# Moving four sums of step 1 from VectorE to GpSimd and to a transfer

## The chip, the cores and the metric

The kernel runs on one NeuronCore of one Trainium2 chip. The metric is the device time of one execution in microseconds. Five engines work side by side, each through its own queue in program order: TensorE (PE in the profile, its weight loads PEld), VectorE (DVE), ScalarE (ACT), GpSimd (POOL) and SyncE (SP), which here only issues transfers. GpSimd issues transfers as well, among them those that add to what stands at their destination. All transfers share 16 transfer engines.

## The reference

```
x_pad = concatenate([zeros((B, K-1, D)), x], axis=1)        # B=8, S=4096, D=192, K=7
out = einsum('hk,bskhg->bshg', softmax(weight), windows(x_pad))   # causal convolution, 8 heads
h = out.reshape(B*S, D) @ w_in                               # 192 -> 2048
g = h * (1 / (1 + exp(-1.702 * h)))
y = g @ w_out                                                # 2048 -> 192
```

A short convolution along the sequence, the same taps for the 24 channels of a head, then two matrix products with a gelu between them, over 32768 tokens, all in float32.

## The kernel before

The tokens are cut into 32 tiles of 1024, one step each (`big` = 0 to 31). Step 0 fills the pipeline and prepares the weights; the loop at the end of the kernel runs steps 1 to 31. Each step has two stages.

`hidden` is the first stage: `h` and its gelu. The blocks of `h` are not computed one by one but from 41 products of sums of blocks of the convolved input with sums of blocks of `w_in`; they are accumulated in four pairs of PSUM banks (`p0` to `p3`), copied, and combined by joins. The order of all this is written out by hand in the list `HIDDEN` (line 737): `mm` is a product (TensorE, L709), `copy` moves a pair of banks (ScalarE L802 or VectorE L804), `join` adds or subtracts two pairs (VectorE, L817), `gelu` writes two rows of `g` (ScalarE, L826 and L833), `early` adds rows of `g` for the next stage. One of the 41 products, `fetch`, already belongs to the next step.

`second` is the second stage: the product with `w_out`, again from sums, of blocks of `g` with sums of blocks of `w_out` (`form`, in `w_out_s` and `w_form`). 25 main products of up to four matmul groups each run one after the other beside side products (TensorE, L1207). Their order stands in `PLAN` (line 1143): `sum` is a sum of blocks of `g` on VectorE (L435 for a plus, L437 for a minus), `acc` the same as an adding transfer from GpSimd's queue (L1183), `seed` and `join` combine results, `tap` multiplies the input of a later step's convolution by one coefficient on ScalarE (L570), `piece` is a piece of the next step's sums of convolved blocks, `turn` and `store` write the output.

The blocks are numbered homes, `spot(i)`: 0 and 1 are the halves of `osbs`, 2 to 4 are rows of `room`, 5 to 20 are the 16 blocks of `g`, each of 128 partitions x 1024 elements. Homes that are free for a while also hold other things: 0 and 1 are `k7` and `k8` of `hidden`, 2 is `k0`.

Some of these sums stand in `hidden` already, in `EARLY_G` (line 1139), which `early(i)` reads; each item is (destination, operand, operation, operand). The last, `(8, 0, "acc")`, is an adding transfer in steps 2 to 31. Step 1 has a list of its own, `EARLY_G_1`, in which that item is a sum on VectorE, so all six are on VectorE in step 1. The places of `early` in `HIDDEN` run 0, 3, 4, then 1 and 5 together, then 2. In `second`, the second `sum` of the plan reads home 8, the fourth main product reads home 0, and the second `side` product, which runs beside it, reads home 1.

Step 1 differs from the later ones. The convolution of its successor's middle third is not finished when it begins: `middle_tap(k)` multiplies one tap on ScalarE (L1096), and a tree of six additions, `middle_pairs`, puts the seven results together. The first addition is on VectorE (L1116), the others are adding transfers (L1114) that `middle_tree(n)` issues, the last two where the third `turn` of `HIDDEN` stands. Work that is to run beside the joins waits in the list `beside`; each join takes one piece from it. Until the third `turn`, `held` keeps back what concerns the next step's convolution (`over`, `ve`, `vc`), in the list `waiting`; then `over` runs, and the rest is released by `last_turn`, the second piece of `beside` after that turn. `ve(i)` is a sum of convolved blocks on GpSimd (L437, `conv_t`), `vc(b)` a copy across partition halves by two transfers from SyncE's queue (L609).

## Time and profile before

| | |
|---|---|
| median of 3 runs | 2263.79 us (2263.47 to 2264.4) |
| the profiled execution's own time | 2263.37 us |
| its span, first to last instruction | 2261.7 us |
| TensorE busy | 2249.5 us |
| VectorE, ScalarE busy | 2112.6, 1714.5 us |
| GpSimd busy | 989.3 us |
| granted TensorE clock | 1.00 |

Every row of the profile says what ran where: start and duration in microseconds, engine, line, operation, the tiles written and read, and in brackets how long the engine had been idle before and what ended that. Matmuls overlap, and their ends are modelled, so a gap in their issue shows only in part as idle time. GpSimd's spans are rough. A view of one engine in the order of time merges neighbours of one kind ("x5"). The first stage of step 1 lies at 93.6 to 136.3 us from the span's start, its second stage at 136.3 to 173.2.

### The profile page before, as it was taken

The numbers are of one execution on the slowest core, as the hardware profiler recorded it, in microseconds if no ns is written. First come the engines' busy times: TensorE is split into PE (matmuls) and PEld (weight loads), VectorE is DVE, ScalarE is ACT, GpSimd is POOL, SyncE is SP. The second block draws the span as 40 slices with busy tenths as digits, with TensorE's granted clock in tenths as the row PEclk, the third lists the DMA queues.
The fourth block names the chain that finished last, engine by engine and source line by source line (L and its number), as shares of the span: only waits on it lengthen the run. The fifth ranks groups of instructions, "written<-read, shape, count | busy, mean of one in ns | idle before, by whom it ended". The sixth has DMA issues, their size and how long they took to land.

```text
span 2261.7 us, 63910 instructions
## 1 busy us (share of the span) xinstructions
PE 2249.5 (99%) x25090; PEld 1348.2 (60%) x25090; DVE 2112.6 (93%) x3266; ACT 1714.5 (76%) x3342; POOL 989.3 (44%) x1013
## 2 busy tenths in 40 slices
PE   9999999999999999999999999999999999999999
PEld 5455655666656666566665566665666656666655
DVE  8999999999999999999999999999999999999998
ACT  8777787777877777777778777777777877777844
POOL 1544454354543444544445434454344454344510
PEclk9999999999999999999999999999999999999999
DMA  9997768866778767787666886677876768765743
GB/s 205 181 173 144 147 134 162 160 139 138 143 150 169 142 138 146 140 165 152 138 141 136 159 164 141 136 144 147 172 142 138 148 134 165 157 137 113 138 96 71
DMA packets 340988, 330.45 MB, mean 146 GB/s; under 512 B 130161, under 2 KB 279281, under 8 KB 340689
## 3 DMA queue, kind: packets, MB, share of 16 engines
q0 software_dynamic: 66928, 168.65, 42.3%
q1 hardware_dynamic: 272112, 157.32, 30.3%
q8 instruction: 199, 3.26, 0.6%
q14 instruction: 101, 0.82, 0.1%
q10 hardware_dynamic: 1648, 0.39, 0.1%
HBM read 53.15 MB, written 25.17 MB: 35 GB/s over the span
## 4 chain that ended last, share of the span: by engine, by line
PE 96%; DVE 2%; ACT 1%; DMA 1%; issue 0%; POOL 0%; SPq 0%; DVEq 0%; ACTq 0%; POOLq 0%
PE slot L709 37%; PE slot L1207 28%; PE sums L1207 17%; PE sums L709 13%; PE slot L987 1%; DVE g L437 0%; DMA g<-g 0%; PE sums L992 0%; DVE g L817 0%; PE slot L992 0%; DMA xin<-in_x_dram 0%; ACT g L833 0%; DVE xt L518 0%; ACT g L826 0%; DVE room L437 0%
## 5 line engine op out<-in xcount | busy, mean ns | idle before, releaser
L709 PE MATMUL slot<-conv_t,w_in_s 64*128 64x512 f32 x3372 | 826.6, 593 | 1.3 <-ACT slot L802 0.7
L1207 PE MATMUL slot<-g,w_form 128*32 128x256 f32 x5872 | 713.5, 379 | 0.0
L709 PEld LDWEIGHTS slot<-conv_t,w_in_s 64*128 64x128 f32 x3372 | 451.1, 187 | 285.2 <-issue 178.6
L437 DVE TENSOR_TENSOR g<-g 128x1024 f32<-128x1024 f32 x372 | 445.0, 1224 | 9.2 <-ACT g L833 1.9
L1207 PE MATMUL sums<-g,w_form 128*32 128x256 f32 x3800 | 422.0, 379 | 0.0
L1207 PEld LDWEIGHTS slot<-g,w_form 128*32 128x32 f32 x5872 | 365.3, 110 | 89.4
L826 ACT ACTIVATE g<-slot 128x512 f32<-128x512 f32 x494 | 265.1, 625 | 127.9 <-PE slot L709 126.5
L709 PE MATMUL sums<-conv_t,w_in_s 64*128 64x512 f32 x1284 | 350.1, 593 | 0.5 <-ACT osbs L802 0.3
L1207 PE MATMUL slot<-g,w_out_s 128*32 128x256 f32 x4080 | 321.5, 380 | 2.4 <-DVE g L437 1.7
L1183 POOL DMA_DIRECT2D g<-g x124 | 116.4, 939 | 441.7 <-PE slot L1207 302.9
L1232 ACT COPY room<-slot 32x256 f32<-32x256 f32 x434 | 158.5, 365 | 188.7 <-PE slot L1207 174.6
L570 ACT ACTIVATE g<-xt,cw 128x512 f32<-128x512 f32 x389 | 270.3, 719 | 4.8 <-PE slot L992 0.4
L437 POOL TENSOR_TENSOR conv_t<-conv_t 128x256 f32<-128x256 f32 x209 | 195.5, 953 | 156.9 <-PE slot L709 90.6
L1207 PEld LDWEIGHTS sums<-g,w_form 128*32 128x32 f32 x3800 | 211.7, 110 | 69.3
L1207 PEld LDWEIGHTS slot<-g,w_out_s 128*32 128x32 f32 x4080 | 166.1, 110 | 128.5 <-ACT g L826 11.4
L915 POOL TENSOR_TENSOR conv_t<-conv_t,g 128x512 f32<-128x512 f32 x174 | 238.6, 1392 | 4.5
L709 PEld LDWEIGHTS sums<-conv_t,w_in_s 64*128 64x128 f32 x1284 | 171.9, 187 | 106.0 <-issue 58.2
L833 ACT ACTIVATE g<-g 128x1024 f32<-128x1024 f32 x155 | 170.7, 1101 | 0.0
L915 POOL TENSOR_TENSOR g<-g 128x512 f32<-128x512 f32 x87 | 110.7, 1273 | 122.7 <-ACT g L570 120.5
L1232 ACT COPY room<-sums 32x256 f32<-32x256 f32 x217 | 79.3, 366 | 103.6 <-PE sums L1207 91.4
L709 PE MATMUL slot<-g,w_in_s 64*128 64x512 f32 x556 | 150.6, 590 | 0.2 <-DVE slot L817 0.2
L826 ACT ACTIVATE g<-sums 128x512 f32<-128x512 f32 x188 | 103.9, 616 | 58.0 <-PE sums L709 57.5
(254 smaller groups left out, 3912.2 us busy)
## 6 DMA issues: line engine op xcount, KB each, us to landing
g<-g POOLq DMA_DIRECT2D x124, 512.0 KB, 6.5
conv_t<-conv_t SPq DMA_DIRECT2D x844, 64.0 KB, 2.0
xin<-in_x_dram SPq DMA_DIRECT2D x240, 180.0 KB, 6.2
out_dram<-osbs SPq DMA_DIRECT2D x183, 128.0 KB, 2.5
g<-g POOLq DMA_DIRECT2D x65, 256.0 KB, 6.7
g<-g SPq DMA_DIRECT2D x248, 64.0 KB, 3.6
g<-room POOLq DMA_DIRECT2D x31, 512.0 KB, 6.0
g<-osbs POOLq DMA_DIRECT2D x30, 512.0 KB, 6.4
```

The lines of the kernel that those rows point to most:

```text
L437: eng.tensor_sub(v(dst), v(a), v(b))
L570: act.mul(home, conv_src(big, c, k), cw[:, c, k : k + 1])
L709: nc.tensor.matmul(slot[h], w_in_s[halves[h], a, v * P : (v + 1) * P], src, start=first, stop=True, skip_group_check=True,)
L826: act.activation(dst[:, :, h, :], ot(bank(src, h)), AF.Gelu_apprx_sigmoid, scale=float(sign))
L833: act.activation(dst.rearrange("p o h t -> p h o t"), src, AF.Gelu_apprx_sigmoid, scale=float(sign))
L915: (vec if eng == "v" else nc.gpsimd).tensor_add(dst, dst, home)
L987: nc.tensor.matmul(chunk(bank, c), w[:, chunk_cols(c)], t, start=first and i == 0, stop=not more and i == len(steps) - 1, skip_group_check ...
L1183: nc.gpsimd.dma_start(out=spot(dst), in_=spot(a), accum_op=ALU.add)
L1207: nc.tensor.matmul(dst, w, t, start=first, stop=last, skip_group_check=True)
L1232: act.copy(to, d)
```

## The change

All of it concerns step 1 (`big == 1`) alone.

- The sum into home 6 (`early(0)`) is issued behind the join into `o10` instead of ahead of it.
- The sum into home 0 (`early(3)`) stays on VectorE. Behind it, the sum into home 8, which was the last but one on VectorE, becomes an adding transfer from home 0.
- The sum into home 2 (`early(4)`) and the two into home 1 (`early(1)`, `early(2)`) go to GpSimd.
- Of the tree's last two additions, which are transfers, one is issued at the third turn as before and the other three pieces of `beside` later. On GpSimd's queue the order is thus: transfer of the tree, transfer into home 8, sum into home 2, last transfer of the tree, two sums into home 1, then the five sums of convolved blocks.
- The held work (`ve`, `vc`) is released when `HIDDEN` is through, instead of within `last_turn`.
- The taps 2 and 3 of the middle third, and with them the addition on VectorE behind tap 3, are issued behind ScalarE's copy of `p3` into `p2`, instead of during the joins ahead of it.

The order of the instructions on TensorE and on SyncE is the same in both kernels; VectorE has four fewer, GpSimd four more.

```diff
@@ copy @@
             if eng == "v" and after_copy:
                 after_copy.pop(0)()
+            if (dst, src) == ("p2", "p3"):
+                while late_taps:
+                    middle_tap(late_taps.pop(0))
@@ join @@
+            if big == 1 and dst == "o10":
+                sum_g(*LATE_G_1)
             seen_joins.append(0)
@@ turn @@
                 held.append(0)
-                middle_tree(2)
+                middle_tree(1)
                 next_turn()
 
-                def last_turn():
-                    next_turn()
-                    held.clear()
-                    while waiting:
-                        waiting.pop(0)()
-
-                beside.extend([next_turn, last_turn, lambda: need("forms")])
+                def last():
+                    need("forms")
+                    middle_tree(1)
+
+                beside.extend([next_turn, next_turn, last])
@@ early @@
-            for item in (EARLY_G if big > 1 else EARLY_G_1)[i]:
-                sum_g(*item)
+            if big > 1:
+                for item in EARLY_G[i]:
+                    sum_g(*item)
+            else:
+                for eng, *item in EARLY_G_1[i]:
+                    sum_g(*item, eng=eng)
@@ hidden, at its end @@
-        assert not beside
+        assert not beside and not late_taps
+        held.clear()
+        while waiting:
+            waiting.pop(0)()
@@ second_first @@
                 sums_w_in(FETCH[0], 3 + 2 * j, 5 + 2 * j)
-                if 0 < j <= K:
+                if j in (3, 4):
+                    late_taps.append(j - 1)
+                elif 0 < j <= K:
                     middle_tap(j - 1)
@@ the lists @@
-    EARLY_G_1 = EARLY_G[:5] + [[(8, 8, "+", 0)]]
+    EARLY_G_1 = [
+        [], [(nc.gpsimd, 1, 7, "-", 6)], [(nc.gpsimd, 1, 1, "-", 11)],
+        [(vec, 0, 5, "+", 6), (None, 8, 0, "acc")], [(nc.gpsimd, 2, 9, "-", 0)], [],
+    ]
+    LATE_G_1 = (6, 6, "-", 10)
@@ sum_g @@
-    def sum_g(dst, a, op, b=None):
+    def sum_g(dst, a, op, b=None, eng=None):
 
         if op == "acc":
             nc.gpsimd.dma_start(out=spot(dst), in_=spot(a), accum_op=ALU.add)
         else:
-            add_up(spot, dst, a, op, b)
+            add_up(spot, dst, a, op, b, eng=eng or vec)
```

More of the change, by code (lines that the diff above doesn't have):

```diff
@@ L1084, in more @@
                 sums_w_in(FETCH[0], 3 + 2 * j, 5 + 2 * j)
-                if 0 < j <= K:
+                if j in (3, 4):
+                    late_taps.append(j - 1)
+                elif 0 < j <= K:
                     middle_tap(j - 1)
             beside.append(more)
-    after_copy, beside = [], []
+    after_copy, beside, late_taps = [], [], []
     MIDDLE = ((14, 0), (11, 2), (3, 0), (17, 2), (3, 2), (11, 2))
```

## The prediction, as it stood before the changed kernel was run

> **What bounds the kernel now.** I read the page first, then the stretches of single stages, then the order of time of each engine around step 1, and the chain that ended last there.
>
> ```profile
> span 2261.7 us, 63910 instructions
> PE 2249.5 (99%) x25090; PEld 1348.2 (60%) x25090; DVE 2112.6 (93%) x3266; ACT 1714.5 (76%) x3342; POOL 989.3 (44%) x1013
> ```
>
> TensorE sets the time: it is busy for 99% of the span. An edit can win only where TensorE stands still, so the next view cuts the span at the stage borders (first the products through L709, then those through L1207) of step 1, and of steps 2 and 3 for comparison.
>
> ```profile
> 93.60:136.28 42.68, 41.19 (x167) 1.00 0.98 185
> 136.28:173.18 36.90, 34.47 (x626) 1.00 1.00 191
> 209.30:243.11 33.81, 33.81 (x626) 1.00 0.98 181
> 243.11:278.75 35.64, 35.64 (x169) 1.00 0.52 115
> ```
>
> The columns are the stretch, its length, TensorE's busy time and matmuls, the granted clock (1.00 throughout) and the transfers' share and rate. A later first stage takes 35.64 us, 41 products and half of one at the border, so 0.859 us a product; that of step 1 takes 42.68, 7.0 more. A later second stage takes 33.81; that of step 1 takes 36.90, 3.1 more. These 10.1 us are all that step 1 can give. Where they lie, by the idle time in brackets:
>
> ```profile
> 112.85 5.55 PE L709 MATMUL slot<-conv_t,w_in_s 64*128 64x512 f32 x23 [0.68 <-ACT slot L802]
> 119.88 4.76 PE L709 MATMUL slot<-conv_t,w_in_s 64*128 64x512 f32 x19 [0.19 <-ACT g L826]
> 129.92 3.44 PE L709 MATMUL slot<-conv_t,w_in_s 64*128 64x512 f32 x12
> 132.90 1.30 PE L709 MATMUL sums<-conv_t,w_in_s 64*128 64x512 f32 x3
> 140.84 0.42 PE L1207 MATMUL slot<-g,w_out_s 128*32 128x256 f32 x3 [0.91 <-DVE g L437]
> 142.59 1.91 PE L1207 MATMUL sums<-osbs,w_form 128*32 128x256 f32 x32
> 145.32 0.42 PE L1207 MATMUL slot<-g,w_out_s 128*32 128x256 f32 x3 [0.82 <-DVE g L437]
> 171.31 0.42 PE L1207 MATMUL slot<-g,w_out_s 128*32 128x256 f32 x3 [0.70 <-DVE room L435]
> ```
>
> The three waits of the second stage make its 3.1 us: about 1.1, 1.1 and 0.9, each some 0.2 over its bracket, because a matmul's modelled end hides the first part of a gap.
>
> **The taps behind the copy.** ScalarE's order was tap (110.03), gelu, a second such tap, copy (112.21):
>
> ```profile
> 110.03 0.73 ACT L1096 ACTIVATE g<-xt,cw 128x512 f32<-128x512 f32 x1
> 110.65 1.05 ACT L833 ACTIVATE g<-g 128x1024 f32<-128x1024 f32 x1
> ...
> 112.21 1.07 ACT L802 ACTIVATE slot<-slot 128x512 f32<-128x512 f32 x2
> ...
> 118.22 2.09 ACT L826 ACTIVATE g<-slot 128x512 f32<-128x512 f32 x4
> ...
> 135.16 2.06 ACT L826 ACTIVATE g<-slot 128x512 f32<-128x512 f32 x4
> ```
>
> With both taps after it, the copy starts at 111.0, 1.2 earlier, and TensorE's product at 112.85 starts near 111.6. The taps still lie ahead of the same gelu, so from 113.2 on ScalarE is where it was, and TensorE's wait at 119.88 is for the gelus that start at 118.22: there the 1.2 us are given back. The addition at L1116 on VectorE now waits for the late tap and pushes the join behind it by 0.43, which VectorE's idle 0.78 before 115.38 takes up (without that cover it would cost 0.43). I put this edit at 0.
>
> **The sums on VectorE.**
>
> ```profile
> 115.38 1.30 DVE L817 TENSOR_TENSOR sums<-osbs,g 128x512 f32<-128x512 f32 x2 [0.78 <-ACT g L826]
> 118.40 1.23 DVE L437 TENSOR_TENSOR g<-g 128x1024 f32<-128x1024 f32 x1 [0.59 <-ACT g L833]
> 126.20 1.18 DVE L435 TENSOR_TENSOR osbs<-g 128x1024 f32<-128x1024 f32 x1
> 131.05 1.19 DVE L437 TENSOR_TENSOR room<-g,osbs 128x1024 f32<-128x1024 f32 x1
> 132.16 1.29 DVE L817 TENSOR_TENSOR sums<-g,room 128x512 f32<-128x512 f32 x2
> 134.55 1.22 DVE L437 TENSOR_TENSOR osbs<-g 128x1024 f32<-128x1024 f32 x1
> 135.69 1.75 DVE L435 TENSOR_TENSOR g<-g,osbs 128x1024 f32<-128x1024 f32 x1
> 137.36 1.76 DVE L437 TENSOR_TENSOR osbs<-osbs,g 128x1024 f32<-128x1024 f32 x1
> 139.04 7.49 DVE L437 TENSOR_TENSOR g<-g 128x1024 f32<-128x1024 f32 x5
> ```
>
> The sum at 118.40 goes behind the join that followed it. Both orders stand idle until about 118.4, once for the gelu and once for the product that the join reads, so it is worth 0, or 0.1.
>
> The sum at 131.05 leaves: the join behind it starts 1.11 earlier. TensorE's three products from 129.92 should end at 132.50 and the next one starts at 132.90; it waits for that join. Gain 0.4, and the second stage starts at 135.9.
>
> The sums at 134.55, 135.69 and 137.36 leave: 4.5 us. VectorE is through its last join at 133.4 and then waits for the gelu whose two halves are the first half of the row at 135.16: until 136.2, less the 0.4, so 135.8. The five sums could start 3.2 earlier than 139.04, the waits at 140.84 and 145.32 would be gone, and the stage would come 2 to 3 us shorter. That is the gain to be had; what follows is what it costs elsewhere.
>
> **What GpSimd gets.** Its queue, with the moved work to come between the first two rows (a transfer, a sum) and after the second (two sums), ahead of the five sums of `conv_t`:
>
> ```profile
> 126.75 0.86 POOL L1114 DMA_DIRECT2D room<-room  x1 [4.68 <-issue]
> 130.57 0.86 POOL L1114 DMA_DIRECT2D conv_t<-room  x1 [2.96 <-issue]
> 135.19 7.86 POOL L437 TENSOR_TENSOR conv_t<-conv_t 128x256 f32<-128x256 f32 x5 [3.77 <-DMA xin<-in_x_dram]
> 143.09 0.87 POOL L1183 DMA_DIRECT2D g<-g  x1
> ```
>
> The groups of GpSimd's sums from step 2 on (the first number behind the bar is the busy time, the second the mean in ns), and the page's median from issue to landing of a transfer of 512 KB:
>
> ```profile
> L915 POOL TENSOR_TENSOR g<-g 128x512 f32<-128x512 f32 x87 | 110.7, 1273 | 122.7 <-ACT g L570 120.5
> L437 POOL TENSOR_TENSOR g<-conv_t 128x256 f32<-128x256 f32 x30 | 22.0, 734 | 6.6 <-PE slot L1207 6.6
> ```
> ```profile
> g<-g POOLq DMA_DIRECT2D x124, 512.0 KB, 6.5
> ```
>
> No row has a GpSimd sum of 1024 elements. One of 256 takes 0.73, one of 512 takes 1.27, so 0.54 for each further 256: 2.4 for 1024, if nothing disturbs it. Beside VectorE's sums the five of 256 took 7.86, near 1.7 each once VectorE's sums are under way, and VectorE's took 1.75 instead of 1.2: 1.7 is VectorE's 1.15 (a sum's way to the next start, 1.11 at 131.05) and GpSimd's 0.55 one after the other. If a long sum suffered in proportion, 2.3 times, it would take 5.6. I take 2.4, with one such sum standing in VectorE's way, because most of VectorE's work in these microseconds has an operand in PSUM or is idle time.
>
> [...]
>
> So: the transfer g<-osbs is issued when the sum at 126.20 is done, 127.4; the first sum runs 128.6 to 131.0, the transfer conv_t<-room follows, the second sum waits for the join of two SBUF operands until 132.3 and ends at 134.6, the third at 137.0. The transfer (6.5 us to landing) has landed by 134.5, before the second of VectorE's five sums needs it. The product at 142.59 reads the third sum; it comes at 141.1 now, 4 us of cover. VectorE's first sum ends at 138.1, the fourth at 143.2; TensorE wants that at 142.8 and waits 0.4. GpSimd's five sums end at 138.1 + 0.55 + 4 x 1.7 = 145.5, not 143.05; with 2.4 us sums everywhere and no contest it would be near 141, in proportion throughout near 155. SyncE's copies of `conv_t` wait for these sums and go with them; they are wanted only in step 2.
>
> **Who waits for GpSimd.** The transfer at 143.09 goes behind those five sums. The chain that ended last in step 1:
>
> ```profile
> 156.20 10.28 DMA g<-g
> 166.60 0.43 DVE g L437
> ```
>
> A transfer issued at 156.20 lands 10.28 us later; VectorE waits for it, TensorE's wait at 171.31 is 4.7 behind that, the end of the stage 1.9 more. So the end hangs on this landing, and 10.28 against a median of 6.5 says that it stood in line:
>
> ```profile
> 142.00:144.00 2.00, 2.00 (x44) 1.23 (x40) 2.00 (x2) 0.64 (x2) 1.92 (x2) 1.00 0.36 88
> 144.00:146.00 2.00, 1.18 (x25) 0.44 (x20) 1.97 (x3) 1.34 (x3) 0.00 (x0) 1.00 0.87 168
> 148.00:150.00 2.00, 2.00 (x44) 1.23 (x40) 2.00 (x3) 1.39 (x3) 0.86 (x1) 1.00 0.64 150
> ```
>
> The second number from the right is the share of the 16 transfer engines: 0.36 with SyncE's copies alone, 0.87 once the transfer of 143.09 moves (some 1.5 us after its issue), full from 150 on. Unused from 142 to 150 (146 to 148 counted as full): 2 x (0.64 + 0.13 + 0.36) = 2.3 us. Afterwards the same bytes have to pass. With the issue at 145.5 and its bytes from 147.0, 5.0 x 0.64 = 3.2 us stay unused, after which the line is full, since VectorE and ScalarE are early and issue is no limit: the landing comes 0.9 later, and the stage ends 0.9 later, whatever TensorE and VectorE won before it. The balance is at an issue near 144.0 (3.5 x 0.64 = 2.3); 1.6 us later costs another 1.
>
> **Sum.** 2263.4 (the profiled execution's own time, span 2261.7) + 0.9 = 2264.3; the median of the runs, 2263.79, lies 0.4 above that execution, so 2264.7.
>
> **Rivals.** *The line of transfers doesn't decide.* If the long sums pass quicker and GpSimd issues by 141 to 143, or the copies' delay thins the line, the landing moves with VectorE: 1 to 2.6 us earlier, at most all of 0.4 + 3.1 = 3.5. For it: 4 us of cover on the third sum, and a full second stage of 33.81 in step 2 with the same transfers. Against it: the two-fold slowing that the rows show just here. About 2.2 won, 2261.6.
>
> *GpSimd becomes the bound.* Should the three long sums end after 141.1, TensorE waits at the product that reads the third. At that point the five short sums end at 149.6 and the line starts at 151.1: 9.1 x 0.64 - 2.3 = 3.5 us lost; at 5.6 us a sum, 146.3, it is 5.2 on that wait and up to 9 at the end. For it: the 1.7 in place of 0.73; against it: VectorE's idle time and PSUM joins beside them. About 5 lost, 2268.8.
>
> *The change moves work but nothing on the path*, the gain in the first stage swallowed at the end of the second and the line as before: 2263.8. This lies within the forecast's own range.
>
> **How the numbers follow.** The forecast, with its neighbour of no effect, 0.53 (2263.2 to 2266.3); the gain, 0.31; GpSimd as the bound, 0.16. The range 2261.2 to 2267.8 holds the first, some two thirds of the second and a third of the third. A change of 0.2%, about 4.5 us, is what a measurement here can tell from none. A gain over 4.5 exceeds the 3.5 worked out: 0.03. A loss over it needs the worse half of the third case and a little besides: 0.12. Within: 0.85.
>
> **What would show it.** TensorE's idle before 140.84 gone and that before 145.32 at most 0.4; the one at 119.88 unchanged; the second stage starting at about 135.9; GpSimd's long sums at 2.4 to 3.4; the transfer now at 143.09 issued near 145.5, and VectorE waiting several microseconds, not 1.1, for the landing near 167.4. Wrong would be a second stage of 34 us without that wait (the gain), a long idle time of TensorE at a product that reads `osbs` (GpSimd), or stalls in step 2, which I take as unchanged.

## The result and the profile after

The changed kernel takes 2267.69 us (median of 22 runs, 2266.71 to 2270.22), the kernel before 2263.83 (median of 22 runs beside it, 2262.76 to 2265.32). The ratio of the means is 1.0019, with a 95% interval of 1.0013 to 1.0026: slower, by 3.9 us between the medians. The 22 times of the changed kernel lie in two groups, 14 from 2266.71 to 2267.96 and 8 from 2269.18 to 2270.22; the profiled execution is of the first, and what the others lose besides isn't shown by any trace. The forecast was 2264.7. Unless another kernel is named, "after" is the changed kernel and all times in us count from the start of the span of the profiled execution; that of after has a span of 2266.0 and a time of 2267.71, 4.34 more than that of before. In after's numbering the copy is still L802, the join is L820, the gelus are L831 and L838, the tree's transfers L1126, the accumulating transfers L1199, the second stage's products L1223.

The stages first: the first stage of step 1 from its second product, its second stage, and a piece of the first one. The columns are the stretch, its length, the busy time of TensorE, its weight loads, VectorE, ScalarE and GpSimd with their instructions, then the granted clock and the share and rate of the transfers.

```profile
93.52:143.29 49.77, 44.29 (x167) 22.94 (x164) 43.40 (x77) 37.82 (x70) 28.14 (x28) 0.97 1.02 193
143.29:177.09 33.80, 33.80 (x625) 20.17 (x624) 30.78 (x48) 24.71 (x52) 11.21 (x13) 1.00 0.93 178
...
138.60:142.00 3.40, 2.92 (x8) 1.38 (x9) 1.61 (x3) 0.81 (x2) 3.40 (x5) 0.50 1.16 220
```

The second stage got all that was to be had there: 33.80 instead of 36.90, 3.1 won. The first stage lost 7.1 (42.68 before). The first stage of step 2 is 0.5 shorter (35.64 against 36.12); a first stage much later in the span is 0.9 longer; the rest is alike to a tenth of a microsecond. 7.1 - 3.1 - 0.5 + 0.9 = 4.4, the difference of the two profiled times.

Where the first stage stood still, in TensorE's order of time:

```profile
111.54 2.46 PE L709 MATMUL slot<-conv_t,w_in_s 64*128 64x512 f32 x8
...
117.73 2.04 PE L709 MATMUL slot<-conv_t,w_in_s 64*128 64x512 f32 x7 [0.98 <-ACT osbs L802]
...
131.27 3.44 PE L709 MATMUL slot<-conv_t,w_in_s 64*128 64x512 f32 x12
136.33 1.12 PE L709 MATMUL sums<-conv_t,w_in_s 64*128 64x512 f32 x2 [1.63 <-DVE sums L820]
139.08 1.22 PE L709 MATMUL sums<-conv_t,w_in_s 64*128 64x512 f32 x1 [1.63 <-DVE sums L820]
```

The product that reads the join `sums<-g,room` waits twice, once for each half of it. The three products from 131.27 should end at 133.85; the next starts at 136.33. VectorE's row of that join, then GpSimd's order:

```profile
132.40 6.63 DVE L820 TENSOR_TENSOR sums<-g,room 128x512 f32<-128x512 f32 x2
```
```profile
129.82 2.69 POOL L437 TENSOR_TENSOR room<-g,osbs 128x1024 f32<-128x1024 f32 x1
132.13 1.21 POOL L1126 DMA_DIRECT2D conv_t<-room  x1
132.73 2.98 POOL L437 TENSOR_TENSOR osbs<-g 128x1024 f32<-128x1024 f32 x1
135.79 2.68 POOL L437 TENSOR_TENSOR osbs<-osbs,g 128x1024 f32<-128x1024 f32 x1
138.43 3.91 POOL L437 TENSOR_TENSOR conv_t<-conv_t 128x256 f32<-128x256 f32 x5
148.99 0.87 POOL L1199 DMA_DIRECT2D g<-g  x1 [6.65 <-PE slot L1223]
```

The join took 1.29 before and takes 6.63. GpSimd's second long sum ends at 132.73 + 2.98 = 135.71, its third at 138.47; each half of the join is done 0.57 behind one of these ends, and a matmul follows 0.05 later. Two of the expectations below call that exclusion. While GpSimd's first long sum ran, VectorE's join that reads one operand from PSUM (`slot<-slot,room`, at 130.54) took its usual 1.27. The chain that ended last goes through this join, too.

From 138.60 to 142.01 TensorE's clock was at half (the row 138.60:142.00 above, 0.50). From 139.08 on, pairs of matmuls came every 0.85 or more instead of 0.43: four such steps took 3.26, to 142.34, instead of 1.72, which costs another 1.5. The first stage of before shows 1.00 throughout.

The remaining 1.35 were lost earlier. TensorE's product at 117.73 waits for ScalarE's copy `osbs<-slot`, which before ran at 115.71 without a wait:

```profile
117.09 1.07 ACT L802 COPY osbs<-slot 128x512 f32<-128x512 f32 x2 [1.35 <-PE slot L709]
```
```profile
L1149 SPq DMA_DIRECT2D out_dram<-osbs x3: 315/586/1158, 106.2 to 108.4; - x3
...
DMA to landing us min/median/max: 3.6/6.1/8.5
```

The second fence is the view of the tile `osbs` between 104 and 119 us: its transfers with the first and the last start, and their time to landing. The TensorE product that the copy reads had ended long before, so the releaser named is not the true one. The copy overwrites `osbs`, which SyncE's three transfers to `out_dram` read. In before they land 4.3 to 4.9 us after their issue, in after 3.6 to 8.5; the one that takes 8.5 is the last, which starts at 108.4, so it lands at 116.9, just ahead of the copy.

From 131.27 to its end the first stage of after takes 12.02 us; in before the same work, from 129.92 on, took 6.36. Of the 5.7 lost here the clock has 1.5; the other 4.2 are the two gaps, beyond the 0.4 that before lost at this place.

### The profile page after: what moved, and what is told of

It is laid out like the page before. It is cut to its first block, busy times and chain, and to the rows that moved or that the text cites. A ratio compares the mean times of both kernels' runs of the same rounds, so it can differ in the third digit from the quotient of the medians.

```text
span 2266.0 us, 63915 instructions
## 1 busy us (share of the span) xinstructions
PE 2252.9 (99%) x25090; PEld 1350.1 (60%) x25090; DVE 2111.7 (93%) x3262; ACT 1715.2 (76%) x3342; POOL 993.2 (44%) x1017
## 3 DMA queue, kind: packets, MB, share of 16 engines
q8 instruction: 199, 3.26, 0.6%
## 4 chain that ended last, share of the span: by engine, by line
PE 94%; DMA 2%; DVE 2%; issue 1%; ACT 0%; SPq 0%; POOL 0%; DVEq 0%; POOLq 0%
PE slot L709 35%; PE slot L1223 29%; PE sums L1223 17%; PE sums L709 12%; DMA g<-g 1%; DMA g<-in_moe_w_in_dram 1%; DMA w_form<-w_out_s 0%; DMA w_form<-w_form 0%; SPq L340 0%; DVE sums L820 0%; DVE xt L518 0%; POOL g L600 0%; POOL conv_t L600 0%; DMA conv_t<-g 0%; SPq L99 0%
## 5 line engine op out<-in xcount | busy, mean ns | idle before, releaser
L1223 PE MATMUL slot<-g,w_form 128*32 128x256 f32 x5872 | 713.0, 379 | 0.0
L1223 PE MATMUL sums<-g,w_form 128*32 128x256 f32 x3800 | 422.0, 379 | 0.0
L1223 PEld LDWEIGHTS slot<-g,w_form 128*32 128x32 f32 x5872 | 364.4, 110 | 89.8
L831 ACT ACTIVATE g<-slot 128x512 f32<-128x512 f32 x494 | 265.2, 625 | 128.2 <-PE slot L709 126.8
L1223 PE MATMUL slot<-g,w_out_s 128*32 128x256 f32 x4080 | 321.3, 379 | 0.0
L1199 POOL DMA_DIRECT2D g<-g x124 | 116.2, 937 | 452.8 <-PE slot L1223 300.4
L1248 ACT COPY room<-slot 32x256 f32<-32x256 f32 x434 | 158.4, 365 | 186.2 <-PE slot L1223 172.2
L1223 PEld LDWEIGHTS sums<-g,w_form 128*32 128x32 f32 x3800 | 211.1, 110 | 69.5
L1223 PEld LDWEIGHTS slot<-g,w_out_s 128*32 128x32 f32 x4080 | 166.2, 110 | 125.4 <-ACT g L831 11.4
L838 ACT ACTIVATE g<-g 128x1024 f32<-128x1024 f32 x155 | 170.6, 1101 | 0.0
L831 ACT ACTIVATE g<-sums 128x512 f32<-128x512 f32 x188 | 104.0, 615 | 63.6 <-PE sums L709 59.9
```

The costliest lines, as they stand in the source:

```text
L831: act.activation(dst[:, :, h, :], ot(bank(src, h)), AF.Gelu_apprx_sigmoid, scale=float(sign))
L838: act.activation(dst.rearrange("p o h t -> p h o t"), src, AF.Gelu_apprx_sigmoid, scale=float(sign))
L1199: nc.gpsimd.dma_start(out=spot(dst), in_=spot(a), accum_op=ALU.add)
L1223: nc.tensor.matmul(dst, w, t, start=first, stop=last, skip_group_check=True)
L1248: act.copy(to, d)
```

## The experiments

Twelve kernels, each against the kernel before on the same chip. The first column of numbers is the median, then the ratio to before with its 95% interval, then the join `sums<-g,room` and the end of the second stage of step 1 in the profiled execution:

```
                        median us   ratio (95%)                join us   stage ends
before                  2263.5-2263.95                           1.29      173.18
after                   2267.69     1.0019 (1.0013 to 1.0026)    6.63      177.09
e1_home1_vec            2263.84     1.0002 (0.9993 to 1.0010)    2.57      175.63
e2_quarters             2272.23     1.0035 (1.0022 to 1.0047)   10.93      182.65
e3_taps_alone           2263.20     0.9997 (0.9988 to 1.0006)    1.29      173.16
e4_home1_gps_alone      2266.94     1.0013 (1.0005 to 1.0022)    1.29      177.91
e5_transfer_alone       2263.16     0.9999 (0.9990 to 1.0008)    1.29      172.85
e6_conv_vec             2262.53     0.9996 (0.9987 to 1.0005)    1.29      173.18
e7_pairs                2269.73     1.0027 (1.0016 to 1.0037)    3.58      179.97
e8_tree_first           2263.73     1.0000 (0.9991 to 1.0009)    1.29      172.31
e9_no_issue_ahead       2267.64     1.0017 (1.0007 to 1.0027)    2.35      178.02
e10_less_line           2262.92     0.9996 (0.9987 to 1.0006)    1.29      172.09
e11_no_transfer         2263.35     1.0000 (0.9991 to 1.0008)    1.29      172.87
e12_issue_behind        2269.87     1.0027 (1.0017 to 1.0037)    5.73      178.54
```

### e1: the two sums into home 1 back on VectorE

```
-        [], [(nc.gpsimd, 1, 7, "-", 6)], [(nc.gpsimd, 1, 1, "-", 11)],
+        [], [(vec, 1, 7, "-", 6)], [(vec, 1, 1, "-", 11)],
```

> The changed kernel with its two long sums into home 1 (`osbs<-g`, `osbs<-osbs,g`) back on VectorE behind its last join; the sum into home 2 stays on GpSimd, the sum into home 8 stays a transfer. Theory (a join of two SBUF operands stands for one whole GpSimd sum in each of its halves): the join `sums<-g,room` takes 1.3 us again instead of 6.63, TensorE's gaps of 2.6 and 2.7 us in front of the last products of the first stage are gone, the granted clock stays 1.00, the second stage stays near 33.8 to 34.3 (it was 36.90 before, 33.80 after), since the two sums fit into VectorE's wait for the last gelus. Time 2260.3 (2263.8 less 0.4 and 3.1) to 2261.8 (if the 1.35 us at the copy `osbs<-slot` come again). Rival (the loss of 3.9 us comes from the moved taps, or from transfers that land later, and the long join only fills time that was lost already): 2264 or more, with TensorE still waiting somewhere near 136 to 139.

The loss is gone: no difference to before. GpSimd's one long sum that is left still holds the join, whose first half was ready at 131.3 and is done 0.56 behind that sum's end at 132.61. VectorE's and GpSimd's rows:

```profile
131.21 2.57 DVE L820 TENSOR_TENSOR sums<-g,room 128x512 f32<-128x512 f32 x2
```
```profile
129.73 2.88 POOL L437 TENSOR_TENSOR room<-g,osbs 128x1024 f32<-128x1024 f32 x1
...
139.10 7.89 POOL L437 TENSOR_TENSOR conv_t<-conv_t 128x256 f32<-128x256 f32 x5 [5.66 <-DMA conv_t<-room]
146.93 0.87 POOL L1199 DMA_DIRECT2D g<-g  x1
```

The clock stays at 1.00. The time missed its 2260.3 to 2261.8, though: VectorE's five sums start at 137.34, 1.7 earlier than before, and the stage doesn't win it. In this execution (span 2264.0, so some 2 us over the runs' median) the sums of `conv_t` wait for the tree's last transfer, the accumulating transfer behind them goes at 146.93 instead of 143.09, and the chain that ended last goes through one transfer, 2.45 later than the 166.48 of before:

```profile
155.44 13.49 DMA g<-g
```

So the loss of after is the join that waits for GpSimd, as the theory had it, and in this execution the gain that should then show is taken by the line of transfers.

### e2: the same two sums in quarters

```
+            cuts = 4 if dst == 1 and eng is nc.gpsimd else 1
+            n = NG // cuts
+            for q in range(cuts):
+                add_up(lambda s: spot(s)[:, q * n : (q + 1) * n, :], dst, a, op, b, eng=eng or vec)
```

> The changed kernel with each of GpSimd's two long sums into home 1 cut into four of 256 elements. Theory (the join's half waits for the one GpSimd instruction under way, and gets its turn behind it): the join `sums<-g,room` takes 1.3 plus at most 2 x 0.75, so 2 to 2.8 us instead of 6.63, the clock stays 1.00, the first stage comes 3.5 to 5 us shorter than the changed kernel's 50.7, time 2262 to 2264. Rival (GpSimd holds VectorE off for as long as it has sums queued, whatever their length): the join still takes 5 to 7 us and the time is 2267 to 2268.5. Rival 2 (no exclusion, the join waits for data or a buffer): unchanged at 6.6 us, 2267.7.

The theory as written fell: shorter instructions made it worse. The first half of the join stood from 132.41 to 142.74, through all thirteen sums that GpSimd had in its queue, of which the last ended at 142.17:

```profile
132.41 10.93 DVE L820 TENSOR_TENSOR sums<-g,room 128x512 f32<-128x512 f32 x2
```
```profile
132.13 1.20 POOL L1126 DMA_DIRECT2D conv_t<-room  x1
132.74 3.37 POOL L437 TENSOR_TENSOR osbs<-g 128x256 f32<-128x256 f32 x4
135.47 3.33 POOL L437 TENSOR_TENSOR osbs<-osbs,g 128x256 f32<-128x256 f32 x4
138.19 3.98 POOL L437 TENSOR_TENSOR conv_t<-conv_t 128x256 f32<-128x256 f32 x5
```

The rows overlap: the first four quarters last from 132.74 to 136.11, and the next row starts at 135.47, 0.64 earlier; so does the third. GpSimd's next sum always started before the last had ended, and VectorE got in behind the last of them only: its first half was done 0.57 after that sum's end. In before the same five sums of `conv_t` took turns with VectorE's sums (7.86 for the five). The rival, that a queued row of GpSimd holds VectorE off, is right here, and not there.

### e7 and e9: what opens the row

In e7 each quarter of the first sum is followed by the quarter of the second that reads its result; GpSimd has to wait for itself after every other sum.

```
...
+        for q in range(4):
+            cut = lambda s: spot(s)[:, q * n : (q + 1) * n, :]
+            add_up(cut, 1, 7, "-", 6, eng=nc.gpsimd)
+            add_up(cut, 1, 1, "-", 11, eng=nc.gpsimd)
```

> The changed kernel with GpSimd's two long sums into home 1 cut into four quarters of 256 elements as in the run with quarters, but in pairs: each quarter of the first sum is followed at once by the quarter of the second that reads its result, so that GpSimd has to wait for itself after every other instruction. Theory (VectorE's join gets in where GpSimd's row of sums has a gap; in the run with quarters there was no gap and the first half stood for 10.33 us, until the last of 13 sums): the first half of the join stands for one or two quarters, 0.7 to 2 us, the second half as much; the join takes 2 to 4.5 us, not 10.93; time 2262.5 to 2267. Rival (the length of GpSimd's row counts, gaps or none; or the transfer issued just ahead of it): the join takes 8 to 11 us again and the time is 2270 or more.

```profile
130.64 3.58 DVE L820 TENSOR_TENSOR sums<-g,room 128x512 f32<-128x512 f32 x2
```
```profile
128.06 2.87 POOL L437 TENSOR_TENSOR room<-g,osbs 128x1024 f32<-128x1024 f32 x1
130.64 1.13 POOL L1128 DMA_DIRECT2D conv_t<-room  x1
131.25 1.27 POOL L437 TENSOR_TENSOR osbs<-g 128x256 f32<-128x256 f32 x1
132.60 1.06 POOL L437 TENSOR_TENSOR osbs<-osbs,g 128x256 f32<-128x256 f32 x1
```

The join takes 3.58, as expected of a row with gaps: its first half is let in at 132.52, when the first quarter has ended and the second waits for its result (the gap is 0.08), and from then on the two engines take turns. That the first half was not let in at 130.93, at the end of the sum into home 2, with the next records (a transfer's issue at 130.64, a sum at 131.25) overlapping, fits too: in e1, where no sum followed the issue, it was. The time, 2269.73, is above the 2267 of the theory, for the reason that e1 showed: the sums of `conv_t` end near 149.1, the accumulating transfer goes at 149.04, and VectorE gets the last landing only at 172.2.

In e9 the same quarters as in e2 are in the same order, but no transfer is issued for a microsecond ahead of them, nor between them; the sum into home 2 is on VectorE.

```
                     need("forms")
-                    middle_tree(1)
...
+        if big == 1:
+            middle_tree(1)
+            sum_g(8, 0, "acc")
...
-        [(vec, 0, 5, "+", 6), (None, 8, 0, "acc")], [(nc.gpsimd, 2, 9, "-", 0)], [],
+        [(vec, 0, 5, "+", 6)], [(vec, 2, 9, "-", 0)], [],
...
```

> The run with quarters, but with the sum into home 2 on VectorE, and the tree's last transfer and the transfer `g<-osbs` issued behind the eight quarters, so that GpSimd issues no transfer for some 3 us ahead of the first quarter; the quarters themselves are the same and no quarter of the first sum waits for another. In the run with quarters their records overlap by 0.65 each (next start 0.68 behind the last, duration 1.3), and the row began while GpSimd was still issuing a transfer. Theory A (the row's overlap comes from the transfer issued right ahead of it; without it GpSimd's sums follow one another by 0.04 and VectorE gets its turn after each): VectorE's sum `room<-g,osbs` and the join's halves stand for one quarter each, 0.5 to 0.8; the join takes 2 to 2.8 us. Theory B (a row of ready sums keeps VectorE out to its end, whatever went before): the first instruction of VectorE with two SBUF operands that comes into the row stands until its end, 3 to 5 us. The time itself suffers from the late tree transfers in both, 2265 to 2272.

```profile
131.42 1.27 DVE L437 TENSOR_TENSOR room<-g,osbs 128x1024 f32<-128x1024 f32 x1
132.62 2.35 DVE L820 TENSOR_TENSOR sums<-g,room 128x512 f32<-128x512 f32 x2
```
```profile
126.45 0.86 POOL L1128 DMA_DIRECT2D room<-room  x1 [3.99 <-issue]
128.45 3.16 POOL L437 TENSOR_TENSOR osbs<-g 128x256 f32<-128x256 f32 x4 [1.14 <-DVE slot L820]
131.58 4.66 POOL L437 TENSOR_TENSOR osbs<-osbs,g 128x256 f32<-128x256 f32 x4
```

Now the records follow one another by 0.03 (128.45 + 3.16 = 131.61 against 131.58), and VectorE gets its turn after each: each half of the join takes 1.22, one quarter longer than alone. Theory A holds for quarters: this row, which doesn't begin under a transfer's issue, has no overlap beyond 0.03, and VectorE gets in. The long sum ahead of the quarters is gone here as well, so e9 doesn't separate the issue from that sum. (The time is that of the late tree: the fourth sum's transfer lands late, and VectorE waits 5.19 for it.)

### e12: the transfer between the long sums

```
                     need("forms")
-                    middle_tree(1)
...
+        if big == 1:
+            middle_tree(1)
```

> The changed kernel with one thing moved: the tree's last transfer (`conv_t<-room`), which stands between GpSimd's long sum into home 2 and those into home 1, is issued behind all three long sums. Theory (a transfer issued between two GpSimd sums joins them to one row that keeps VectorE's join out to its end; sums without it follow one another by 0.04 us and let VectorE in after each): the join's first half gets in at the end of the sum into home 2, near 132.5, instead of standing for the whole next sum (until 136.28); its second half stands for one long sum, until 135.5 or so: the join takes 3 to 4 us, not 6.63, and TensorE's two gaps in front of the last products become one of 2 to 2.7. The transfer is issued near 137.5 to 138, six microseconds late, so the sums of `conv_t` start at 141 to 145 and the second stage pays for it: 2265.5 to 2270 in all. Rival (the long sums alone keep VectorE out): the join takes 6 to 7 us again.

```profile
132.46 5.73 DVE L820 TENSOR_TENSOR sums<-g,room 128x512 f32<-128x512 f32 x2
```
```profile
129.32 0.86 POOL L1200 DMA_DIRECT2D g<-osbs  x1 [1.29 <-DVE osbs L435]
129.88 2.69 POOL L437 TENSOR_TENSOR room<-g,osbs 128x1024 f32<-128x1024 f32 x1
132.21 2.66 POOL L437 TENSOR_TENSOR osbs<-g 128x1024 f32<-128x1024 f32 x1
134.95 2.68 POOL L437 TENSOR_TENSOR osbs<-osbs,g 128x1024 f32<-128x1024 f32 x1
```

A miss: the first half stood through the whole second sum again and was done 0.57 behind its end (132.21 + 2.66 = 134.87), the second half behind the third. The other transfer, `g<-osbs`, still runs into the first sum (129.32 + 0.86 = 130.18 against 129.88), and the second sum starts 0.36 before the first has ended: the overlap is passed on from the first to the second, without a transfer between them. Which of the two transfers starts it didn't matter here (5.73 against 6.63); the third sum, which reads the second's result, starts 0.08 after its end, and there VectorE gets in. Taking only one of the transfers away leaves the loss.

### e3: the taps alone

```
+            if (dst, src) == ("p2", "p3"):
+                while late_taps:
+                    middle_tap(late_taps.pop(0))
...
-                if 0 < j <= K:
+                if j in (3, 4):
+                    late_taps.append(j - 1)
+                elif 0 < j <= K:
...
```

> The kernel before with the moved taps alone (taps 2 and 3 behind ScalarE's copy of p3 to p2). Theory (the prediction's step 1, an edit worth nothing; the 1.35 us that the changed kernel loses at the copy `osbs<-slot` are the late landing of the output's transfer from `osbs`, which has nothing to do with the taps): copy `slot<-slot` near 111.0, TensorE's product that stood at 112.85 near 111.6, TensorE's product that stood at 119.88 not moved by more than 0.1 if the landing comes in time, time 2263.6 to 2264.0, no difference. Rival (the taps' new place makes the copy late): copy at 117, product at 121.2, time 2265.1 or so, slower by 0.06%.

TensorE's product comes at 111.32 instead of 112.85, and the wait at 119.88 is there as before:

```profile
111.32 6.77 PE L709 MATMUL slot<-conv_t,w_in_s 64*128 64x512 f32 x23
...
119.56 2.90 PE L709 MATMUL slot<-conv_t,w_in_s 64*128 64x512 f32 x11 [0.19 <-ACT g L829]
```

ScalarE's copy ahead of both runs 0.3 earlier here (108.76 against 109.07), and so does the second row: the 1.2 that the taps win at the first are given back at the second. The copy `osbs<-slot` runs at 115.40, without a wait. The taps are not what made it late in after: it waited in after, e2, e9 and e12, where the slowest of the three transfers to `out_dram` landed 7.6 to 8.5 us after its issue, and not in e1, e5 and e7, where it landed within 6.6; all of them are the same program up to there. It varies from one execution to the next, and why is open.

### e4: the two sums into home 1 alone

```
-                sum_g(*item)
+                sum_g(*item, eng=nc.gpsimd if big == 1 and i in ON_GPS else None)
...
+    ON_GPS = (1, 2)
...
```

> The kernel before with the two sums into home 1 on GpSimd and nothing else of the change. Theory (exclusion for a whole instruction): the first of them starts while the join `sums<-g,room` is near (131 to 134); one or both halves of it, or of the join behind it, stand for 1.5 to 3 us each, the first stage grows by 2 to 6 us, the second one shrinks by 1.5 to 3, and the clock shows 0.5 for some microseconds if TensorE stands still twice: time 2264 to 2268. Rival (these two sums are harmless, the loss comes from the other parts): VectorE 3 us earlier, the join 1.3 us, 2261 to 2262.

The time is in the theory's range, but by another way, so this run tells nothing of the join (1.29). In the order of before the five sums of `conv_t` stand ahead of the long ones in GpSimd's queue, and they wait for the tree:

```profile
138.12 3.49 POOL L437 TENSOR_TENSOR conv_t<-conv_t 128x256 f32<-128x256 f32 x5 [5.19 <-DMA conv_t<-room]
141.58 2.33 POOL L437 TENSOR_TENSOR osbs<-g 128x1024 f32<-128x1024 f32 x1
```
```profile
147.41 3.19 PE L1208 MATMUL sums<-osbs,w_form 128*32 128x256 f32 x25 [5.93 <-POOL osbs L437]
```

TensorE waits 5.93 at the product that reads `osbs`: the rival "GpSimd becomes the bound", had the long sums come later. It also gives the price of a long sum by itself, 2.33.

### e5, e8, e6, e11, e10: what the gain of the second stage is worth

e5 is after with all three long sums on VectorE; only the fourth stays a transfer.

```
-        [], [(nc.gpsimd, 1, 7, "-", 6)], [(nc.gpsimd, 1, 1, "-", 11)],
-        [(vec, 0, 5, "+", 6), (None, 8, 0, "acc")], [(nc.gpsimd, 2, 9, "-", 0)], [],
+        [], [(vec, 1, 7, "-", 6)], [(vec, 1, 1, "-", 11)],
+        [(vec, 0, 5, "+", 6), (None, 8, 0, "acc")], [(vec, 2, 9, "-", 0)], [],
```

> The changed kernel with all three long sums back on VectorE; only the fourth stays a transfer (`g<-osbs`), and the taps and the sum behind the join stay moved. Theory (a GpSimd sum that reads SBUF holds up the join of two SBUF operands; behind it, the end of the second stage hangs on the line of transfers and so on when GpSimd's five sums of `conv_t` are done): the join `sums<-g,room` takes 1.3 us, its two halves 0.7 each; VectorE's five sums start 1.5 to 1.8 us earlier than 139.04; TensorE's waits at 140.84 and 145.32 shrink to 0.3 each; the five sums of `conv_t` still alternate with VectorE's at 1.7 us each, the transfer behind them is issued at 143 to 145, and the end of the stage wins nothing: time 2263 to 2264.5, no difference to before. Rival (the transfers do not set the end): what the two waits lose, the whole stage wins, 2261 to 2262.

```profile
131.33 1.29 DVE L820 TENSOR_TENSOR sums<-g,room 128x512 f32<-128x512 f32 x2
...
136.19 8.46 DVE L437 TENSOR_TENSOR g<-g 128x1024 f32<-128x1024 f32 x5
```
```profile
154.51 11.65 DMA g<-g
```

The second view is the chain that ended last. VectorE's five sums start 2.85 earlier than before, the join is undisturbed, and the stage ends at 172.85 against 173.18, because the last transfer lands at 166.16 against 166.48. e8 puts the tree's two last transfers back ahead of the new one (`middle_tree(2)` at the turn):

> As the run with the transfer alone, with the tree's two last transfers in their old order ahead of the transfer `g<-osbs` (the other run has that one between them). Theory (the sums of `conv_t` wait for the tree's last landing where it is late, 139.1 in the run with home 1 on VectorE): they start at 135.2 as before, not at 136 to 139, the transfer behind them is issued 1 to 3 us earlier than in the run with the transfer alone, and the time is 0 to 1.5 us less than there, 2262.5 to 2264. Rival (the place between the transfers does not matter): the same as there within 0.3.

GpSimd's sums of `conv_t` start at 135.27 (135.90 in e5), but the issue behind them goes at 143.24 against 143.51, and the time is the same within 0.6: the place is worth nothing that can be told. e6 is e8 with the five sums of `conv_t` on VectorE (`sum_of(big + 1, SUMS_H[i], vec if big == 1 else None)`), e11 is e6 with the fourth sum on VectorE again instead of a transfer:

> As the run with the transfer alone, with the tree's two last transfers in their old order ahead of the transfer `g<-osbs`, and with GpSimd's five sums of `conv_t` in step 1 on VectorE, behind the two sums into home 1. No GpSimd sum is left between 125 and 145 us. Theory: the five take 0.36 each on VectorE (1.8) and every long sum of VectorE takes 1.15 to the next start, not 1.67, so the five sums of `g` start near 138.7 to 139.2 and end at 144.5 to 145, 1.5 to 2 earlier than before; TensorE's waits at 140.84 and 145.32 are 0.3 or less; the transfer that was issued at 143.09 goes at 141.5 to 142.5, the last landing comes 1 to 2.5 us earlier: 2261 to 2262.5. Rival (the sums of `conv_t` wait for a transfer's landing, at 135 before and at 139 in the run with home 1 on VectorE, and VectorE's order is fixed, so its five sums of `g` wait behind them): five sums start at 141 or later, TensorE waits 2 to 3 us at 140.84, 2265 to 2267.

> The kernel before with the moved taps and the sum behind the join, and with GpSimd's five sums of `conv_t` in step 1 on VectorE behind its last sum of `g`; the fourth sum (home 0 into home 8) is on VectorE again, so no transfer is added. Theory (the line sets the end, and 512 KB less in it are worth more than 1.1 us of VectorE): the five sums of `g` start near 139.5 to 140.5, the wait at 140.84 stays at 0 to 1, the one at 145.32 falls to 0.3, and the transfer of 143.09 goes at 141.5 to 143: the stage ends at 171.3 to 172.5, 2261 to 2262.7. Rival (VectorE's five sums start later than 139.04 and TensorE waits there for what it wins at the end): 2263.5 to 2264.5.

```profile
138.00 1.76 DVE L437 TENSOR_TENSOR conv_t<-conv_t 128x256 f32<-128x256 f32 x5
139.68 5.89 DVE L437 TENSOR_TENSOR g<-g 128x1024 f32<-128x1024 f32 x5
```
```profile
155.88 10.63 DMA g<-g
```

These are VectorE's order and the chain of e6. Alone on VectorE the five sums of `conv_t` take 1.76 and the five of `g` 5.89 instead of 7.49, and TensorE's two first waits are gone; the landing at 166.51 is that of before. In this execution of e6 the second stage began at 137.25, 1.0 later than in before, so the stage itself is 1.0 shorter and still ends where it did. e6 has the lowest median of all, 2262.53, and can't be told from before; e11 lies at 2263.35, with about 1 us of TensorE's first wait left. Both miss their theory: e6's last landing is not earlier, and e11's stage ends at 172.87, not at 171.3 to 172.5. No version beats the kernel before by more than its noise.

e10 is e6 without the first of the five accumulating transfers in step 1.

```
-            sum=sum_g, acc=lambda d, a: sum_g(d, a, "acc"), main=begin_main, side=begin_side, go=go, seed=seed,
+            sum=sum_g, acc=lambda d, a: None if big == 1 and d == 14 else sum_g(d, a, "acc"), main=begin_main, side=begin_side, go=go, seed=seed,
```

> The run with the sums of `conv_t` on VectorE, with the first of the second stage's five accumulating transfers (512 KB, `g<-g`, home 13 into home 14) left out in step 1 alone; its sum is missing from the output. In before, and in the runs with the taps alone, the transfer alone, the tree first and the sums of `conv_t` on VectorE, the second stage of step 1 ends at 172.4 to 173.3 whatever VectorE wins before it. Theory (the line of transfers sets that end): 512 KB less at some 190 GB/s is 2.7 us; the last `g<-g` lands 1.5 to 2.7 us earlier, the stage ends at 170.5 to 171.7 (not below 137.3 + 33.8 = 171.1), time 1 to 2.2 us under that run. Rival (a chain of VectorE or TensorE sets the end): stage end and time as there, within 0.4.

A miss. The stage ends at 172.09: 1.1 earlier than in e6, whose second stage also began 0.6 later, but only 0.2 earlier than in e8, which leaves no transfer out. The 1.5 and more that were expected don't show, and the time does not follow either (2262.92). The chain shows what lies behind the end then: two transfers of the next step's tree, one waiting for the other, and behind them the first stage of step 2.

```profile
157.30 9.99 DMA g<-room
...
167.82 6.75 DMA g<-room
```

## Why the prediction was wrong

- **The failed step** is in the part on what GpSimd gets: "the second sum waits for the join of two SBUF operands until 132.3 and ends at 134.6". It was the other way round: the join waited for that sum and then for the third, and its halves were done at 136.28 and 139.03, not by 132.3 (133.7 with the 1.35 that this execution was late); TensorE stood still twice for it. I had weighed such a wait, one long sum standing in VectorE's way, at VectorE's first sum of five, behind the join, and had given the join itself the right of way without a row for it. The 138.1 in the sum, where that first sum ends, holds this wait (GpSimd's third sum to 137.0, then VectorE's 1.1), and no run shows it there: in after VectorE's five start at 143.16, 2.95 of idle time behind a gelu, and take 5.89, and in e1 (137.34) and e5 (136.19) no long sum of GpSimd runs when they start; what the runs showed in its place is the wait of the join, 6.63 in after and 2.57 in e1 instead of 1.29. My reason, that "most of VectorE's work in these microseconds has an operand in PSUM or is idle time", passed over this join, which reads both from SBUF. It was ready at 132.48, in the very moment at which the sum into home 2 ended (132.50), and it feeds TensorE directly. e1 takes the two sums away, and the loss with them.
- **A term was missing:** the clock. Two gaps close behind one another cost a further 1.5 by a clock of 0.50; nothing in the profile of before showed it, and no case of mine had it.
- **GpSimd's long sums** take 2.69, 2.98 and 2.68, and 2.33 undisturbed: the 2.4 that I took, and the 2.4 to 3.4 that I named, were right. The bound of 5.6 in proportion wasn't met. The size of GpSimd's work was not the mistake, the question who waits for whom was.
- **The taps:** right. The product came at 111.54 (I had 111.6), and e3 puts the edit at no difference (0.9988 to 1.0006). The wait at 119.88 stayed, as 0.19 at 121.24.
- **The sum behind the join o10** was put at 0 or 0.1. It was not run by itself; e5, which has it, shows no loss.
- **The sum at 131.05** was to give TensorE 0.4 at 132.90. With that sum on GpSimd (e1) the join was ready 1 us earlier and was held by just that sum until 132.61; TensorE's product came at 133.23. The gain is lost to the engine that took the work over.
- **The second stage:** the 2 to 3 us to be had there are real, 3.1 in after; the second stage of 34 us, which I had named as the sign of the gain, came with a loss because the first stage had paid for it. That they would be swallowed at the end by the line of transfers fits as well: in before, e3, e5, e6, e8 and e11 the stage starts anywhere between 135.45 and 137.25 and VectorE's five sums of `g` between 136.2 and 139.7, and the stage ends at 172.3 to 173.2. The price of a late issue was a little small: at 146.93 (e1) my way of reckoning gives (148.4 - 142) x 0.64 - 2.3 = 1.8, and the landing came 2.45 late. After itself does not show the line at work, since its second stage began 7 us late, when GpSimd's sums of `conv_t` were already done (142.34); the issue at 148.99 waited for TensorE, not for GpSimd. That this line sets the end is argued from the chains and these ends; e10, which was to show it, doesn't: with 512 KB less the stage ends 0.2 to 1.1 earlier by the run that it is set beside.
- **The rival with GpSimd as the bound** had about the size (5 lost), by luck, and the wrong place: it put the wait at the product that reads `osbs`, in the second stage, where e4 shows it when the long sums come late. After's wait is at the end of the first stage. A loss in the first stage was not among the cases.
- **The range** 2261.2 to 2267.8 holds the median by a tenth, and by luck: the way in which the time was lost was in none of the cases. Of the 3.9 us, 1.35 in the profiled execution are the late landing at the copy `osbs<-slot`, which is not the change's; the runs don't show how often it comes.

## What to carry to other kernels

Before work goes from VectorE to GpSimd, list every VectorE instruction with two operands in SBUF that falls into the time of the moved sums, and look at who waits for it: here a join that feeds TensorE stood through a whole sum in each of its halves (6.63 instead of 1.29, after), and a row of GpSimd sums that started under the issue of a transfer kept its first half out to the end of the row (e2); cutting the sums smaller made it worse there (10.93 against 6.63), while a row started with no transfer's issue running into it let VectorE in after each (2.35, e9). A sum of 1024 elements cost GpSimd 2.3 to 3.4 us (2.33 and 3.38 in e4) where VectorE needs 1.2, so beside such VectorE work the move can cost more than it frees: one long sum moved won nothing (e1), three lost 3.9 us (after). And when the end of a stage hangs on a line of transfers, ask what time the line would give before you shorten the engines' work: five versions that started VectorE's last sums up to 2.9 us earlier, or sped them up (e1, e5, e6, e8, e11), came out within 0.04% of before, with intervals of 0.09% to either side, which is 2 us.

## What the runs showed of the hardware that was not expected

- Rows of GpSimd sums come in two manners. Where the next record starts 0.03 to 0.06 before the last ends (before, e9), VectorE's instructions with two SBUF operands take turns with them (five sums of each engine in 7.49 and 7.86 in before, 1.22 for each half of the join in e9). Where the next record, a sum or a transfer's issue, starts 0.3 to 0.65 before (after, e2, e7 at its start, e12), the half of VectorE's join that came then stood until a gap, or in e2 to the end of the last sum (10.33): 0.08 was enough, where GpSimd's next sum reads the result of the last (after, e7, e12). Every overlapped row began under the issue of a transfer by GpSimd. In the whole trace of before no sum starts under an issue, and of its 294 pairs of sums that overlap none does so by more than 0.06. But each overlapped row also has a sum of 1024 elements at its head, and no run separates the two. What happens inside GpSimd there isn't to be seen in the trace.
- TensorE's granted clock changed in steps of 3.41 us: in after it was at 1.00 for 133.12 us, at 0.50 for 3.413 and at 1.00 again for 2123.09, which is 39, 1 and 622 times 3.413. It was at 0.50 for 3.41 us in after, e7 and e12, for 6.83 (twice that) in e4 and e9, and for 10.24 (three times) in e2. What went ahead of each is a stretch of 3.41 us in which TensorE was little busy; three such stretches, in after, e12 and e1:

```profile
135.18:138.60 3.42, 1.12 (x2) 0.30 (x2) 3.42 (x2) 0.60 (x1) 3.34 (x3) 1.00 1.09 218
```
```profile
135.61:139.02 3.41, 1.78 (x6) 0.71 (x8) 3.41 (x3) 0.60 (x1) 2.83 (x2) 1.00 1.16 236
```
```profile
171.03:174.44 3.41, 1.79 (x37) 0.81 (x29) 3.34 (x11) 2.08 (x4) 1.04 (x2) 1.00 1.10 200
```

Behind the first two the clock was 0.50, behind the third it stayed at 1.00. The other rows fit: TensorE was busy for 0, 0.44, 1.03 and 1.38 us ahead of the slow stretches of e2, e4, e7 and e9, and for 1.86 in e5 and 1.93 in e1 where the clock stayed. So an estimate from these rows puts the border near 1.8 of 3.41 us here (1.78 in e12, 1.79 in e1), as far as modelled busy times tell; in e1 and e5, where the clock stayed, no change of it marks where a stretch begins. A single pause of some 2 us did not bring the slow clock by itself: those of 1.9 and 2.0 us (from one matmul's start to the next) in e5 and e1 cost no clock, in stretches with 1.86 (e5), 1.79 and 1.93 (e1) busy; after's two, of 2.2 each, fell for the most part into one with 1.12. At half the clock a stretch with 2.74 busy (e2, 142.12:145.53) was followed by another at 0.50, one with 2.93 (after, 138.60:142.01) by 1.00. The stretches lie differently in each execution (135.18 in after, 135.61 in e12), so the same pause need not cost the same each time.
